# A decode attention block on one core: the query matrix to the head of SP's queue, x to ACT's, and half of one value set to GpSimd's queue

## The chip, the core and the metric

The kernel runs on one core of a Trainium2 chip. The metric is the device time of one execution in microseconds, where lower is better. A run of the profiler adds a record of every instruction, every DMA packet and every semaphore increment of one execution.

## The reference, cut to what matters

```python
def _A_ref(x, k_cache, v_cache, wq, wo):      # B=8, Sq=1, D=512, Hq=32, Hkv=8, Sk=4096, Dh=128
    W = min(4096, max(256, Sk // 4))          # 1024: the last 1024 positions alone
    q = (x @ wq).reshape(B, Sq, Hq, Dh).transpose(0, 2, 1, 3)
    k = jnp.repeat(k_cache[:, :, Sk - W:, :], rep, axis=1)     # rep = 4
    v = jnp.repeat(v_cache[:, :, Sk - W:, :], rep, axis=1)
    p = _softmax(jnp.einsum("bhqd,bhkd->bhqk", q, k) * (Dh ** -0.5), axis=-1)
    o = jnp.einsum("bhqk,bhkd->bhqd", p, v)
    return o.transpose(0, 2, 1, 3).reshape(B, Sq, Hq * Dh) @ wo
def _B_ref(x, w_gate, w_up, w_down):          # F = 1792
    return (_gelu(x @ w_gate) * (x @ w_up)) @ w_down

xn = _layernorm(A_x)
return A_x + _A_ref(xn, ...) * _silu(_B_ref(xn, ...))
```

All inputs are bf16. The attention window is 1024 positions of 8 batches and 8 key heads, so that keys and values are 16 MB each, `wq` and `wo` 4 MB each, and the three matrices of the feed-forward part 5.25 MB together.

## The kernel before, in words

The work is one pass over 47.46 MB that is read from HBM once. All large loads go through SP's queue, in the order in which the program issues them, into a ring of 19 slots of 1 MB (`slot`, 8 KB in each of 128 partitions). The order is: `x_sb`; four row blocks of `wq`; two of `w_gate` and two of `w_up`; the key sets K0 to K2; two halves of `w_down`; then V0, K3, V1, K4 and so on to V15 (`seq`, lines 404 to 415); and at the end `wo` in seven pieces of 512 KB and two of 256 KB (`load_wo`). A set is one key head and four batches, loaded as 32 groups of 32 positions by 4 batches (`load_set`, line 102), so 16 sets of keys (K) and 16 of values (V).

The first stage is the layer norm of x (lines 176 to 196: statistics on VectorE, a square root on ScalarE, four transposes on TensorE), then the query product (line 209) and the gate and up products (line 227). The main loop walks the key sets in quarters: transposes of the keys (line 289), copies out of PSUM by VectorE or ScalarE (lines 294, 296), scores (line 306), the maximum, the exponentials, the sums and the value product (line 368), each some steps behind the other. The last stage multiplies with `wo` (line 476), gates, adds x and stores four pieces.

x is read a second time, by four small loads of 8 rows by 128 columns each in ACT's queue (`xq_sb`, line 84). Only the last addition (line 486) uses it. GpSimd issues no DMA; it prepares constants by `select` (line 139) and is idle from 6 us on.

Completion semaphores are given out by the framework: eight for the DMAs of SP and ACT together, in the order of the program. A DMA waits until the one eight places before it has landed, and a load into a reused slot also waits for TensorE to have read it. So up to eight loads are under way at a time.

Of the kernel before, what the change touches and what calls it, by code (L numbers as in the profile page):

```python
# [11 lines left out]
BF16 = mybir.dt.bfloat16  # L12
# [5 lines left out]
def kernel(  # L18
# [13 lines left out]
    nc = tc.nc  # L32

    B, Sq, D = A_x.shape
    Hkv, Sk, Dh = A_k_cache.shape[1], A_k_cache.shape[2], A_k_cache.shape[3]
# [3 lines left out]
    win0 = Sk - W  # L39
    F = B_w_gate.shape[1]  # L40
    NDC = D // 128
    NFC = F // 128
    scale = float(Dh) ** -0.5
    P = nc.NUM_PARTITIONS
# [3 lines left out]
    G = 4  # L48
    NB = B // G
    NS = Hkv * NB  # L50
    KP = P // G
# [5 lines left out]
    NQB = D // 128  # L57
# [8 lines left out]
    rows = ctx.enter_context(tc.tile_pool(name="rows", bufs=1))  # L66
# [9 lines left out]


    x_sb = rows.tile([B, D], BF16, name="x_sb")
    nc.sync.dma_start(out=x_sb, in_=A_x.flatten_outer_dims())
    xq_sb = rows.tile([P, 128], BF16, name="xq_sb")  # L80
    nc.gpsimd.memset(xq_sb, 0.0)
    x_flat = A_x.flatten_outer_dims()
    for q in range(NQB):
        nc.scalar.dma_start(
            out=xq_sb[32 * q : 32 * q + B, :],
            in_=x_flat[:, q * 128 : (q + 1) * 128],
        )

    def slot():
        return ring.tile([P, SET], BF16, name="slot")  # L90

    def load_rows(w, r0, n, per, name):

        t = slot()
        cols = w.shape[1]
        nc.sync.dma_start(
            out=t[:, 0 : n * cols],
            in_=w.rearrange("(p k) n -> p k n", p=P)[:, r0 : r0 + n, :],
        )
        return t[:, 0 : n * cols].rearrange("p (k n) -> p k n", k=n)  # L100

    def load_set(cache, s):
        h, b0 = s // NB, (s % NB) * G
        t = slot()
        nc.sync.dma_start(
            out=t,
            in_=cache[b0 : b0 + G, h, win0:Sk, :].rearrange(
                "g (p c) d -> p g (c d)", p=KP
            ),
        )  # L110
        return t.rearrange("p (c d) -> p c d", c=NCH)

    def load_wo(h, r0, n):

        t = slot()
        nc.sync.dma_start(
            out=t[:, 0 : n * D],
            in_=A_wo[h * rep * Dh : (h + 1) * rep * Dh, :].rearrange(
                "(p r) n -> p r n", r=rep
            )[:, r0 : r0 + n, :],  # L120
        )
        return t[:, 0 : n * D].rearrange("p (r n) -> p r n", r=n)


    ident = consts.tile([P, P], BF16, name="ident")
# [31 lines left out]
    for r in range(rep):  # L157
        t = consts.tile([P, P], BF16, name=f"pick{r}")
# [3 lines left out]
    for i in range(3):  # L162
        t = consts.tile([P, NC], BF16, name=f"shift{i}")
# [17 lines left out]
    nc.vector.memset(eps_sb, 1e-5)  # L181
    rstd = rows.tile([B, 1], FP32, name="rstd")
    nc.scalar.activation(out=rstd, in_=mv[:, 1:2], func=ACT.Sqrt, bias=eps_sb, scale=1.0)
    nc.vector.reciprocal(out=rstd, in_=rstd)
    xhat = rows.tile([B, D], BF16, name="xhat")
    nc.vector.tensor_scalar(
        out=xhat, in0=x_sb, scalar1=mv[:, 0:1], scalar2=rstd[:, 0:1],
# [16 lines left out]

    q_ps = ps_sc.tile([P, Hq, B], FP32, name="sc")
    for k in range(NDC):
        w = load_rows(A_wq, k, 1, NDC, "wq")
        for m in range(Hq):
            nc.tensor.matmul(  # L209
                q_ps[:, m, :], w[:, 0, m * Dh : (m + 1) * Dh], xnT[:, k, :],  # L210
                start=(k == 0 and m == 0), stop=(k == NDC - 1 and m == Hq - 1),
                skip_group_check=True,
            )
    nc.vector.tensor_copy(
        out=qT, in_=q_ps.rearrange("p (h j) b -> p h b j", j=rep)
# [68 lines left out]
    K, V, kT, sc, pT, rec = {}, {}, {}, {}, {}, {}  # L284
# [132 lines left out]
    def fetch(kind, s):  # L417
        while True:
            k, i = pending.pop(0)
            if k == "K":  # L420
                K[i] = load_set(A_k_cache, i)
            elif k == "V":
                V[i] = load_set(A_v_cache, i)
            else:
                n = NFC // 2
                down_tiles.append(load_rows(B_w_down, i * n, n, NFC, "wd"))
            if (k, i) == (kind, s):
                return

    LV = 4 * (AHEAD - 1) + 2  # L430
    for t in range(QT * NS + LV + QT + 3):
        s, i = divmod(t, QT)
        if s < NS:
            if i == 0:
                fetch("K", s)
            transpose_quarter(s, i)
# [15 lines left out]
        if 0 <= s3 < NS:  # L452
            if i3 == 0:
                fetch("V", s3)
            value_quarter(s3, i3)
# [16 lines left out]
    for h, r0, n in parts:  # L472
        w = load_wo(h, r0, n)
        for r in range(r0, r0 + n):
            for q in range(NQB):
                nc.tensor.matmul(  # L476
                    s_ps[32 * q : 32 * q + B, :], oR[:, h, r, :],
                    w[:, r - r0, q * 128 : (q + 1) * 128],
                    start=(h == 0 and r == 0), stop=(h == Hkv - 1 and r == rep - 1),
                    skip_group_check=True,  # L480
                )
# [5 lines left out]
    for q in range(NQB):  # L487
        eng = nc.sync if q % 2 == 0 else nc.scalar
        eng.dma_start(
            out=o_flat[:, q * 128 : (q + 1) * 128], in_=out_sb[32 * q : 32 * q + B, :]  # L490
# [31 lines left out]
```

## Time and profile before

| | |
|---|---|
| median of 3 runs | 125.14 us (124.98 to 125.2) |
| the profiled execution | 125.09 us |
| its span in the profile | 123.2 us |
| TensorE, busy | 88.1 us (71%) |
| VectorE, busy | 68.9 us (56%) |
| ScalarE, busy | 45.9 us (37%) |
| GpSimd, busy | 4.9 us (4%) |
| bytes read from HBM | 47.46 MB, 385 GB/s over the span |
| chain that ended last | DMA 71%, TensorE 18%, VectorE 4% |

The span is the time from the first to the last instruction; 1.9 us of the execution lie around it. Times within the profile count from the start of the span. "SPq" and "ACTq" are the sequencers of SP and ACT that issue DMAs; q1 is SP's DMA queue and q10 ACT's. The queues of the kind "instruction" fetch program code. A DMA spreads over up to 16 DMA engines, and each of them adds one to its semaphore when its share has landed.

### The profile page before, as it was taken

The numbers are of one execution on the slowest core, as the hardware profiler recorded it, in microseconds if no ns is written. First come the engines' busy times: TensorE is split into PE (matmuls) and PEld (weight loads), VectorE is DVE, ScalarE is ACT, GpSimd is POOL, SyncE is SP. The second block draws the span as 40 slices with busy tenths as digits, with TensorE's granted clock in tenths as the row PEclk, the third lists the DMA queues.
The fourth block names the chain that finished last, engine by engine and source line by source line (L and its number), as shares of the span: only waits on it lengthen the run. The fifth ranks groups of instructions, "written<-read, shape, count | busy, mean of one in ns | idle before, by whom it ended". The sixth has DMA issues, their size and how long they took to land.

```text
span 123.2 us, 4592 instructions
## 1 busy us (share of the span) xinstructions
PE 88.1 (71%) x2044; PEld 79.1 (64%) x2044; DVE 68.9 (56%) x218; ACT 45.9 (37%) x54; POOL 4.9 (4%) x21
## 2 busy tenths in 40 slices
PE   0154338877995699989697979769889879855840
PEld 0143337876984688979586969658778668644720
DVE  5200100025577557978596879669679697875010
ACT  1300000053674426548254645346545565510000
POOL 7800000000000000000000000000000000000000
PEclk9999999999999999999999999999999999995595
DMA  3999999999999999999999999999999999999820
GB/s 67 411 426 431 424 410 421 421 415 423 425 420 415 418 412 423 412 418 415 420 420 423 418 415 420 418 415 412 423 418 418 415 423 415 408 398 410 320 92 3
DMA packets 7508, 47.77 MB, mean 388 GB/s; under 512 B 952, under 2 KB 960, under 8 KB 2880
## 3 DMA queue, kind: packets, MB, share of 16 engines
q1 hardware_dynamic: 7392, 47.46, 93.7%
q8 instruction: 16, 0.26, 0.9%
q14 instruction: 4, 0.03, 0.1%
q10 hardware_dynamic: 96, 0.01, 0.1%
HBM read 47.46 MB, written 0.01 MB: 385 GB/s over the span
## 4 chain that ended last, share of the span: by engine, by line
DMA 71%; PE 18%; DVE 4%; issue 3%; SPq 1%; DVEq 0%
DMA slot<-in_A_k_cache_dram 33%; DMA slot<-in_A_wo_dram 22%; DMA slot<-in_B_w_up_dram 12%; PE kT_ps L289 8%; DMA slot<-in_A_wq_dram 4%; PE sc L306 3%; PE o_ps L368 3%; PE sum_ps L351 1%; PE m_ps L322 1%; PE sc L340 1%; DVE kT L294 1%; PE s L265 1%; DVE mx L315 1%; DVE rec L356 1%; DVE oR L398 1%
## 5 line engine op out<-in xcount | busy, mean ns | idle before, releaser
L289 PE MATMUL kT_ps<-ident,slot 128*128 128x128 bf16 x512 | 40.8, 226 | 6.1 <-DMA slot<-in_A_k_cache_dram 5.1
L296 ACT ACTIVATE kT<-kT_ps 128x1024 bf16<-128x1024 bf16 x32 | 32.7, 1023 | 23.9 <-PE kT_ps L289 22.3
L289 PEld LDWEIGHTS <-slot 128*128 128x128 bf16 x512 | 31.0, 100 | 7.4 <-DMA slot<-in_A_k_cache_dram 5.8
L368 PEld LDWEIGHTS <-slot 128*128 128x128 bf16 x512 | 20.5, 96 | 10.4 <-issue 5.7
L294 DVE COPY kT<-kT_ps 128x1024 bf16<-128x1024 bf16 x32 | 21.6, 675 | 8.1 <-PE kT_ps L289 8.1
L368 PE MATMUL o_ps<-pT,slot 128*128 128x16 bf16 x512 | 22.0, 170 | 2.6 <-DVE oT L374 1.2
L306 PE MATMUL sc<-qT,kT 128*128 128x16 bf16 x512 | 22.7, 170 | 0.7 <-issue 0.6
L306 PEld LDWEIGHTS <-kT 128*128 128x128 bf16 x512 | 19.9, 97 | 0.9 <-issue 0.8
L346 ACT ACTIVATE pT<-sc 128x512 bf16<-128x512 f32 x16 | 9.6, 597 | 16.0 <-PE sc L340 16.0
L315 DVE TENSOR_REDUCE mx<-sc 128x16 f32<-128x512 f32 x16 | 11.1, 691 | 5.6 <-PE sc L306 5.3
L356 DVE TENSOR_REDUCE rec<-sum_ps 128x16 f32<-128x512 f32 x16 | 11.1, 691 | 3.5 <-PE sum_ps L351 3.1
L227 PE MATMUL sc<-xnT,slot 128*128 128x8 bf16 x112 | 7.4, 202 | 3.6 <-DMA slot<-in_B_w_gate_dram 2.9
L227 PEld LDWEIGHTS <-slot 128*128 128x128 bf16 x112 | 7.1, 161 | 3.9 <-DMA slot<-in_B_w_gate_dram 3.1
L238 ACT ACTIVATE z<-sc 128x112 f32<-128x112 f32 x1 | 0.3, 264 | 21.4 <-PE sc L227 21.4
L209 PE MATMUL sc<-xnT,slot 128*128 128x8 bf16 x128 | 4.1, 168 | 5.3 <-DMA slot<-in_A_wq_dram 5.3
L209 PEld LDWEIGHTS <-slot 128*128 128x128 bf16 x128 | 3.7, 104 | 5.7 <-DMA slot<-in_A_wq_dram 5.7
L351 PE MATMUL sum_ps<-pT,ones 128*128 128x512 bf16 x16 | 6.2, 389 | 0.7 <-issue 0.7
L340 PE MATMUL sc<-shift,spread 68*128 68x512 bf16 x16 | 6.0, 376 | 1.0 <-DVE kT L294 0.9
L322 PE MATMUL m_ps<-identf,mx 128*16 128x128 f32 x16 | 4.4, 275 | 2.7 <-DVE kT L294 1.3
L239 DVE TENSOR_SCALAR z<-z 128x112 f32<-128x112 f32 x1 | 0.2, 218 | 10.8 <-ACT z L238 10.8
L398 DVE CAST oR<-m_ps 32x32 bf16<-32x32 f32 x32 | 5.8, 183 | 0.7 <-PE m_ps L388 0.4
L476 PE MATMUL s<-slot,oR 128*8 128x128 bf16 x128 | 3.9, 285 | 2.5 <-DMA slot<-in_A_wo_dram 1.3
(58 smaller groups left out, 47.1 us busy)
## 6 DMA issues: line engine op xcount, KB each, us to landing
slot<-in_A_k_cache_dram SPq DMA_DIRECT2D x16, 1024.0 KB, 20.1
slot<-in_A_v_cache_dram SPq DMA_DIRECT2D x16, 1024.0 KB, 19.8
slot<-in_A_wq_dram SPq DMA_DIRECT2D x4, 1024.0 KB, 7.9
slot<-in_A_wo_dram SPq DMA_DIRECT2D x7, 512.0 KB, 18.6
slot<-in_B_w_gate_dram SPq DMA_DIRECT2D x2, 896.0 KB
slot<-in_B_w_up_dram SPq DMA_DIRECT2D x2, 896.0 KB
slot<-in_B_w_down_dram SPq DMA_DIRECT2D x2, 896.0 KB
slot<-in_A_wo_dram SPq DMA_DIRECT2D x2, 256.0 KB, 9.2
```

Of the source, the lines that this page charges most:

```text
L209: nc.tensor.matmul(q_ps[:, m, :], w[:, 0, m * Dh : (m + 1) * Dh], xnT[:, k, :], start=(k == 0 and m == 0), stop=(k == NDC - 1 and m == Hq ...
L227: nc.tensor.matmul(gu_ps[:, j, w, :], wv[:, k, j, :], xnT[:, k0 + k, :], start=(w == 0 and k0 == 0 and j == 0 and k == 0), stop=(w == 1 an ...
L289: nc.tensor.transpose(ps[:, c * P : (c + 1) * P], K[s][:, i * CQ + c, :], ident)
L294: nc.vector.tensor_copy(out=t, in_=ps)
L296: nc.scalar.activation(out=t, in_=ps, func=ACT.Copy)
L306: nc.tensor.matmul(sc[s][:, i * CQ + c, :], t[:, c * P : (c + 1) * P], q, start=(i == 0 and c == 0), stop=False, skip_group_check=True,)
L315: nc.vector.tensor_reduce(out=m, in_=sc[s].rearrange("p c n -> p n c"), axis=AX.X, op=ALU.max)
L340: nc.tensor.matmul(sc[s].rearrange("p c n -> p (c n)"), spread[0:SHK, :], r[0:SHK, :].unsqueeze(1).to_broadcast([SHK, NCH, NC]), start=Fal ...
L346: nc.scalar.activation(out=t, in_=sc.pop(s), func=ACT.Exp, scale=scale)
L351: nc.tensor.matmul(ps.rearrange("p c n -> p (c n)"), ones, pT[s].rearrange("p c n -> p (c n)"), start=True, stop=True,)
L356: nc.vector.tensor_reduce(out=t, in_=ps.rearrange("p c n -> p n c"), axis=AX.X, op=ALU.add)
L368: nc.tensor.matmul(o_ps[s].rearrange("p g j -> p (g j)"), V[s][:, c, :], pT[s][:, c, :], start=(c == 0), stop=(c == NCH - 1),)
```

## The change

`x_sb` is loaded by ACT instead of SP, so that the first block of `wq` is the first load in SP's queue; all four blocks are issued ahead of the constants. The four loads of `xq_sb`, and the clearing of that tile, come after the square root of the layer norm. V7 is loaded in three pieces instead of one: two loads of 32 partitions in GpSimd's queue, each behind a load of 8 rows by 2 by 64 elements of x into a tile that nothing reads (`turn`), and one load of the other 64 partitions in SP's queue. The large loads of GpSimd wait for the slot of K0 to be free; the value product of set 7 waits for all three.

```diff
-    nc.sync.dma_start(out=x_sb, in_=A_x.flatten_outer_dims())
-    xq_sb = rows.tile([P, 128], BF16, name="xq_sb")
-    nc.gpsimd.memset(xq_sb, 0.0)
-    x_flat = A_x.flatten_outer_dims()
-    for q in range(NQB):
-        nc.scalar.dma_start(
-            out=xq_sb[32 * q : 32 * q + B, :],
-            in_=x_flat[:, q * 128 : (q + 1) * 128],
-        )
+    nc.scalar.dma_start(out=x_sb, in_=A_x.flatten_outer_dims())
...
+    turn = [rows.tile([B, 2, 96], BF16, name=f"turn{i}") for i in range(2)]
+
+    def load_set(cache, s, split=False):
         h, b0 = s // NB, (s % NB) * G
         t = slot()
...
+        src = cache[b0 : b0 + G, h, win0:Sk, :].rearrange(
+            "g (p c) d -> p g (c d)", p=KP
+        )
+        n = 0
+        if split:
+            for i in range(2):
+                m = KP // 4
+                nc.gpsimd.dma_start(
+                    out=turn[i][:, :, 0:64],
+                    in_=x_flat.rearrange("b (i n) -> b i n", i=2)[:, :, 0:64],
+                )
+                nc.gpsimd.dma_start(
+                    out=t[n * G : (n + m) * G, :], in_=src[n : n + m]
+                )
+                n += m
+        nc.sync.dma_start(out=t[n * G : P, :], in_=src[n:KP])
         return t.rearrange("p (c d) -> p c d", c=NCH)
...
+    wq_tiles = [load_rows(A_wq, k, 1, NDC, "wq") for k in range(NDC)]
...
     nc.scalar.activation(out=rstd, in_=mv[:, 1:2], func=ACT.Sqrt, bias=eps_sb, scale=1.0)
+
+    xq_sb = rows.tile([P, 128], BF16, name="xq_sb")
+    nc.gpsimd.memset(xq_sb, 0.0)
+    x_flat = A_x.flatten_outer_dims()
+    for q in range(NQB):
+        nc.scalar.dma_start(
+            out=xq_sb[32 * q : 32 * q + B, :],
+            in_=x_flat[:, q * 128 : (q + 1) * 128],
+        )
...
     for k in range(NDC):
-        w = load_rows(A_wq, k, 1, NDC, "wq")
+        w = wq_tiles[k]
...
             elif k == "V":
-                V[i] = load_set(A_v_cache, i)
+                V[i] = load_set(A_v_cache, i, (k, i) == ("V", 7))
```

More of the change, by code (lines that the diff above doesn't have):

```diff
@@ L100, in load_rows @@
         return t[:, 0 : n * cols].rearrange("p (k n) -> p k n", k=n)
-    def load_set(cache, s):
+    turn = [rows.tile([B, 2, 96], BF16, name=f"turn{i}") for i in range(2)]
+    def load_set(cache, s, split=False):
         h, b0 = s // NB, (s % NB) * G
         t = slot()
[L105 to L109, printed above, removed]
-        )
+        src = cache[b0 : b0 + G, h, win0:Sk, :].rearrange(
+            "g (p c) d -> p g (c d)", p=KP
+        )
+        n = 0
[11 more added lines that the diff above has]
+        nc.sync.dma_start(out=t[n * G : P, :], in_=src[n:KP])
         return t.rearrange("p (c d) -> p c d", c=NCH)
```

## The prediction, made before the changed kernel ran

> **What bounds the kernel now.** I read the DMA part of the page first, then the end of the chain of waits.
>
> ```profile
> DMA  3999999999999999999999999999999999999820
> GB/s 67 411 426 431 424 410 421 421 415 423 425 420 415 418 412 423 412 418 415 420 420 423 418 415 420 418 415 412 423 418 418 415 423 415 408 398 410 320 92 3
> ...
> q1 hardware_dynamic: 7392, 47.46, 93.7%
> q8 instruction: 16, 0.26, 0.9%
> q14 instruction: 4, 0.03, 0.1%
> q10 hardware_dynamic: 96, 0.01, 0.1%
> ```
>
> The DMA engines are full from slice 2 to slice 37: TensorE's 71% costs nothing while data come at this rate. The chain in order of time ends in DMA as well:
>
> ```profile
> 91.77 18.61 DMA slot<-in_A_wo_dram
> ...
> 110.44 8.89 DMA slot<-in_A_wo_dram
> 119.33 0.04 issue
> 119.38 0.31 PE s L476 x8
> ```
>
> So only two things move the end: when the stream starts, and when the last DMA engine finishes. The busy time by stretches says that they don't finish together (the last two columns are DMA share and GB/s):
>
> ```profile
> 110.00:115.00 5.00, 2.33 (x65) 1.99 (x69) 2.70 (x12) 0.00 (x0) 0.00 (x0) 0.55 1.04 410
> 115.00:116.00 1.00, 1.00 (x48) 1.00 (x40) 0.00 (x0) 0.00 (x0) 0.00 (x0) 0.50 0.84 324
> 116.00:117.00 1.00, 0.87 (x40) 0.67 (x32) 0.00 (x0) 0.00 (x0) 0.00 (x0) 0.50 0.60 236
> 117.00:118.00 1.00, 0.40 (x16) 0.20 (x7) 0.00 (x0) 0.00 (x0) 0.00 (x0) 0.86 0.47 180
> 118.00:119.00 1.00, 0.67 (x24) 0.39 (x24) 0.00 (x0) 0.00 (x0) 0.00 (x0) 1.00 0.33 117
> ```
>
> The last load of `wo` shows the same: of its 16 increments nine come at 115.81 to 117.91 us and seven at 118.90 to 119.33.
>
> **Who is late.** The records of single packets tell why. In the steady stream an engine moves 8 KB in 309 ns and its next packet follows within 4 ns, so the packets join into 16 chains. Queue q8's sixteen fetches of 16 KB take 0.96 to 1.11 us each, and the packet behind one mostly takes 0.8 us instead of 0.31: some 1.5 us lost to that engine. They go round eight chains in fixed order (15.1, 25.8, 37.5, 44.9, 50.8, 57.1, 63.4, 69.6 us, then the first again at 75.7). Chains hit twice are late by some 3 us (one load ends at 102.6 to 103.3 us on chains never hit, at 105.7 to 106.2 on those hit twice).
>
> Which eight? An 8-row load runs on eight engines (q10's 96 packets are four loads and two stores, each of 8 data and 8 semaphore packets). The loads of `xq_sb` mark their eight chains at 5.1 to 7.2 us. Followed to the fetches, four of those hit are marked ones and four are not. One of the marked could be swapped with another chain that starts its packets in the same nanoseconds; so it is at least three on each side. Among the late seven at the end are three marked and four others.
>
> **The change, part by part.**
>
> *The start.* The view by time:
>
> ```profile
> 0.73 0.39 SPq L79 DMA_DIRECT2D x_sb<-in_A_x_dram  x1
> 0.96 1.62 ACTq L84 DMA_DIRECT2D xq_sb<-in_A_x_dram  x4
> 1.18 1.93 SPq L96 DMA_DIRECT2D slot<-in_A_wq_dram  x4
> 2.30 0.68 DVE L177 BATCH_NORM_STATS2 stats<-x_sb 8x6 f32<-8x512 bf16 x1 [0.47 <-DMA x_sb<-in_A_x_dram]
> ```
>
> Without the load of x ahead, the first `wq` block is issued at 0.73 instead of 1.18: the stream starts **0.45 us** earlier (bounds 0.39, the issue alone, and 0.45; I take 0.45). Everything behind it in SP's queue moves along.
>
> *x behind `wq`.* ACT issues x at about 0.96, and its packets reach engines that have begun the first `wq` block. The nearest row is the second load of `xq_sb`, issued about 1.36: its packets came only at 5.1, behind that block, and it landed at 5.6 to 6.2. So x lands near 5.7 instead of 2.3. From the statistics to the first query product (6.03) it took 3.73 us, of which 0.7 was ScalarE's table load (2.62 to 3.90), now done under the wait: the product starts near 8.7. Cover: a block takes 1.02 us of TensorE and they land 2.5 us apart, the last at 13.5, or 13.1 now; three before it need 3.1, so a start up to 10.0 costs nothing. Slack 1.3 us: cost 0. Without it each late microsecond delays the gate product, which itself waits 2.7 us for its load: still hidden.
>
> *`xq_sb`.* Its four issues (1.62 us) now stand behind the square root in ACT's queue, near 7; ACT's next work is line 238, at 25 us. Semaphores shift by the new order: gate's first block waits for the first `wq` block (landing near 5.5) with 3 MB still queued, 7.5 us of stream; K0 waits for the first of `xq_sb`, landed by 11, before its turn at 13. The memset of 0.20 on GpSimd moves behind the selects. All 0.
>
> *V7.* SP's piece keeps 64 partitions, 32 KB on each of 16 engines instead of 64 KB. The other 512 KB come from GpSimd when K0's slot is free, at 31 us (the end of its transposes), behind one small load each; SP issued V7 at 52.9, so these are early, and GpSimd has nothing else to do. No row shows a GpSimd DMA. By the nearest rows, the 8-row loads, a load with eight shares uses eight engines: 32 KB each, and both large loads on the same eight if the small ones take the other eight in turn: 64 KB. Then eight engines carry 32 KB more than before, four packets of 309 ns, **+1.24 us**, and eight carry 1.24 us less. The lower bound is 0: both loads spread evenly. Upper: if GpSimd cuts rows into 256-byte packets (15 ns each in q10's rows), 64 KB take 3.84 instead of 2.47 us: +2.6. I take 1.24: 8 KB rows are moved whole everywhere in this trace.
>
> The Trainium skill (DMA: Bandwidth & Descriptors, on why a DMA increments its semaphore by 16) says that a GpSimd DMA with eight shares takes eight consecutive engines from a cursor that goes round. By that rule both large loads do fall on one half; no row here shows it.
>
> With late engines in both halves, the loaded half has them whichever half it is. The end is the latest engine: 119.33 - 0.45 + 1.24 = 120.12, **+0.79 us**. Relief of the other half is worth nothing. From 31 to about 73 us the loaded engines lag by 2.47, so sets land up to 2.0 us later there; eight loads are under way (20 us from issue to landing), so the stream doesn't run dry, and TensorE's delay has until 110 to vanish.
>
> The profiled execution took 125.09, 0.05 under the median of 125.14: 125.09 + 0.79 = **125.9**.
>
> **Rivals.**
>
> 1. *Relief.* The loaded eight are exactly the eight that q8 never hits. Then the late ones end at 119.33 - 1.24 = 118.09, the others at up to 117.51 + 1.24 = 118.75, and the end is 118.75 - 0.45 = 118.30, 1.03 earlier: **124.1**. It decides as soon as no fetched engine is in the loaded half. For it: 512 KB moved is close to what levels 3 us. Against: the marks of `xq_sb`, if GpSimd's eight are cut as ACT's eight are. Chance 0.28.
> 2. *No shift.* GpSimd's loads use all 16 engines or alternate halves; only the start counts: 125.09 - 0.45 = **124.6**. Against: eight leading shares. Chance 0.07. The same skill page, in its section that issuing engines are not separate DMA queues, says that loads from any engine share the same 16 and that a change of issuer saves only issue time; by that the time would be this one, too.
> 3. *Small packets* from GpSimd: +2.6 - 0.45 on late engines, **127.2**. Chance 0.05.
>
> **The numbers.** About 0.2%, 0.25 us, is what can be told from no change. Forecast 0.57, with its own range 125.5 to 126.5 (a lower end if the extra packets fall on engines whose second fetch comes late; the upper if TensorE's delay remains in part). Slower: 0.57 + 0.05 = 0.62. Faster: 0.28 + 0.07 = 0.35. Same: 0.03, where the halves differ by chance. The range 124.0 to 126.5 leaves out the small packets and tails.
>
> **What would show it.** In the profile after: `wq` first in SP's queue at about 0.73; the first query product between 8 and 9.5 with no later wait for it; a third queue with some 64 packets of 8 KB after 31 us; line 476's last wait ending near 120.1, and a DMA share above 0.2 from 118 to 120. I am wrong if the increments of the last `wo` load draw together and end near 118.3 (relief), or keep today's spread 0.45 earlier (no shift); and if the query product ends after the gate blocks are in, the start was not free.

## The result, and the profile after

The changed kernel took **131.4 us** (median of five runs, 131.21 to 131.77) against 125.14 us (124.98 to 125.2) for the kernel before: a ratio of 1.0506, 95% interval 1.0491 to 1.0521. The direction was forecast, the size was not: 6.3 us slower instead of 0.8, far above the range's upper end of 126.5. Its profiled execution took 131.48 us with a span of 129.6.

The page's DMA part shows where. This is the busy share and the rate of the DMA engines in 40 slices of 3.24 us each, and the queues:

```profile
DMA  3999999999999999999999999999999999999510
GB/s 116 430 425 420 416 422 420 417 413 422 386 279 286 351 420 420 415 422 407 417 425 399 240 313 407 422 417 415 420 412 425 410 427 406 407 401 393 228 69 3
...
q1 hardware_dynamic: 7312, 46.93, 91.7%
q0 software_dynamic: 224, 0.53, 1.5%
```

The row of nines is as unbroken as it was before: by the busy share nothing has happened. The row below it has two holes, slices 11 to 14 (386, 279, 286, 351) and 22 to 24 (399, 240, 313). The engines are busy and move less, so in these stretches a packet takes longer. The view by stretches puts them beside TensorE. Behind the stretch and its length stand the busy times of TensorE, of its weight loads, of VectorE, ScalarE and GpSimd; the last three columns are granted clock, DMA share and GB/s:

```profile
20.00:33.00 13.00, 10.78 (x163) 10.37 (x161) 3.68 (x9) 4.52 (x6) 1.66 (x3) 1.00 1.01 419
33.00:46.00 13.00, 6.30 (x113) 5.29 (x110) 5.11 (x15) 4.06 (x5) 0.00 (x0) 0.72 1.02 325
46.00:69.00 23.00, 21.98 (x490) 19.77 (x489) 16.35 (x49) 11.29 (x14) 0.00 (x0) 0.79 1.01 418
69.00:79.00 10.00, 7.83 (x189) 7.08 (x187) 7.42 (x24) 4.86 (x6) 0.00 (x0) 1.00 1.02 318
79.00:110.00 31.00, 27.81 (x640) 25.32 (x639) 24.30 (x77) 16.70 (x20) 0.00 (x0) 0.94 1.01 417
```

The same two stretches of the kernel before, from the same view:

```profile
33.00:46.00 13.00, 10.24 (x243) 9.00 (x241) 8.50 (x24) 6.51 (x8) 0.00 (x0) 1.00 1.02 420
69.00:79.00 10.00, 8.28 (x202) 7.60 (x202) 7.73 (x24) 5.38 (x7) 0.00 (x0) 1.00 1.01 415
```

The first hole holds GpSimd's two loads: the 64 data packets of 8 KB in q0 begin between 34.6 and 43.7 us. The second lies between 71 and 76 us; no packet of q0 is left there, and it fits SP's 64-partition piece of V7, issued at 57.9 us with some 15 to 21 us from issue to landing. Packet by packet, an 8 KB packet that took 309 ns before (the shortest; the median is 312) takes about 540 ns (median from 36.5 to 38 us) and 614 ns (median from 71 to 73 us). I add up what all 8 KB packets took beyond 309 ns and divide by 16 engines: from 33 to 46 us that is 3.10 us against 0.25 before, from 69 to 79 us 2.57 against 0.20. So the two holes cost every engine **2.85 and 2.37 us** on average.

Most of it is paid by other loads. From 69 to 79 us 157 packets took over 400 ns (two before), and the piece of V7 has only 64. From 33 to 46 us 230 did, and GpSimd's 64 packets (mean 446 ns) bear 8.7 of the 49.6 us lost.

The chain in order of time ends as before, in the last piece of `wo`, only later (landing 125.58 instead of 119.33, 6.25 us):

```profile
116.73 8.85 DMA slot<-in_A_wo_dram
125.58 0.04 issue
125.62 0.31 PE s L493 x8
```

This landing can be summed up: 119.33 before, -0.45 for the start, +2.85 and +2.37 for the holes, +1.24 for the unevenly loaded engines gives 125.34; 0.24 is left over. The last load also shows the uneven engines themselves: its 16 increments came within 3.52 us before (115.81 to 119.33) and within 6.02 now (119.56 to 125.58). The end by stretches, same columns as above:

```profile
118.00:119.00 1.00, 1.00 (x26) 0.72 (x27) 0.23 (x1) 0.00 (x0) 0.00 (x0) 0.50 1.01 397
...
120.00:122.00 2.00, 0.85 (x28) 0.82 (x31) 0.94 (x6) 0.00 (x0) 0.00 (x0) 0.50 0.70 272
122.00:124.00 2.00, 2.00 (x84) 1.96 (x73) 0.00 (x0) 0.00 (x0) 0.00 (x0) 0.50 0.38 141
124.00:126.00 2.00, 1.12 (x40) 0.49 (x31) 0.05 (x1) 0.00 (x0) 0.00 (x0) 0.99 0.18 60
```

The start, by time:

```profile
0.74 0.59 ACTq L79 DMA_DIRECT2D x_sb<-in_A_x_dram  x1
0.74 2.05 SPq L88 DMA_DIRECT2D slot<-in_A_wq_dram  x4
...
2.79 0.68 DVE L185 BATCH_NORM_STATS2 stats<-x_sb 8x6 f32<-8x512 bf16 x1 [0.96 <-DMA x_sb<-in_A_x_dram]
...
5.57 1.02 PE L226 MATMUL sc<-xnT,slot 128*128 128x8 bf16 x32 [0.52 <-DMA slot<-in_A_wq_dram]
```

and GpSimd's issues, by time:

```profile
30.80 0.57 POOL L112 DMA_DIRECT2D slot<-in_A_v_cache_dram  x1 [23.89 <-PE kT_ps L306]
31.36 0.55 POOL L108 DMA_DIRECT2D turn<-in_A_x_dram  x1
31.90 0.56 POOL L112 DMA_DIRECT2D slot<-in_A_v_cache_dram  x1
```

### The profile page after: what moved, and what is told of

It reads as the page before. It is cut to its first block, busy times and chain, and to the rows that moved or that the text cites. A ratio compares the mean times of both kernels' runs of the same rounds, so it can differ in the third digit from the quotient of the medians.

```text
span 129.6 us, 4601 instructions
## 1 busy us (share of the span) xinstructions
PE 92.7 (72%) x2044; PEld 83.3 (64%) x2044; DVE 68.7 (53%) x218; ACT 46.0 (35%) x54; POOL 7.2 (6%) x25
## 4 chain that ended last, share of the span: by engine, by line
DMA 58%; PE 28%; DVE 7%; issue 3%; SPq 1%; ACT 0%; DVEq 0%
DMA slot<-in_A_k_cache_dram 36%; PE kT_ps L306 13%; DMA slot<-in_B_w_up_dram 8%; DMA slot<-in_A_wo_dram 7%; DMA slot<-in_A_wq_dram 7%; PE o_ps L385 4%; PE sc L323 4%; PE sc L357 2%; DVE mx L332 2%; DVE kT L311 1%; PE m_ps L339 1%; PE sum_ps L368 1%; PE s L282 1%; DVE rec L373 1%; SPq L88 1%
## 5 line engine op out<-in xcount | busy, mean ns | idle before, releaser
L306 PE MATMUL kT_ps<-ident,slot 128*128 128x128 bf16 x512 | 44.5, 238 | 5.7 <-DMA slot<-in_A_k_cache_dram 3.4
L306 PEld LDWEIGHTS <-slot 128*128 128x128 bf16 x512 | 33.7, 106 | 7.2 <-DMA slot<-in_A_k_cache_dram 3.6
L385 PEld LDWEIGHTS <-slot 128*128 128x128 bf16 x512 | 21.1, 98 | 13.8 <-issue 5.7
L385 PE MATMUL o_ps<-pT,slot 128*128 128x16 bf16 x512 | 22.5, 171 | 6.7 <-DMA slot<-in_A_v_cache_dram 4.6
L323 PEld LDWEIGHTS <-kT 128*128 128x128 bf16 x512 | 20.7, 99 | 0.0
L244 PEld LDWEIGHTS <-slot 128*128 128x128 bf16 x112 | 7.0, 159 | 3.7 <-DMA slot<-in_B_w_gate_dram 2.9
L226 PEld LDWEIGHTS <-slot 128*128 128x128 bf16 x128 | 3.7, 104 | 5.4 <-DMA slot<-in_A_wq_dram 5.4
L368 PE MATMUL sum_ps<-pT,ones 128*128 128x512 bf16 x16 | 6.7, 416 | 0.8 <-issue 0.8
L357 PE MATMUL sc<-shift,spread 68*128 68x512 bf16 x16 | 6.5, 404 | 0.9 <-DVE kT L311 0.8
```

Source lines behind the costliest of these rows:

```text
L226: nc.tensor.matmul(q_ps[:, m, :], w[:, 0, m * Dh : (m + 1) * Dh], xnT[:, k, :], start=(k == 0 and m == 0), stop=(k == NDC - 1 and m == Hq ...
L244: nc.tensor.matmul(gu_ps[:, j, w, :], wv[:, k, j, :], xnT[:, k0 + k, :], start=(w == 0 and k0 == 0 and j == 0 and k == 0), stop=(w == 1 an ...
L306: nc.tensor.transpose(ps[:, c * P : (c + 1) * P], K[s][:, i * CQ + c, :], ident)
L323: nc.tensor.matmul(sc[s][:, i * CQ + c, :], t[:, c * P : (c + 1) * P], q, start=(i == 0 and c == 0), stop=False, skip_group_check=True,)
L357: nc.tensor.matmul(sc[s].rearrange("p c n -> p (c n)"), spread[0:SHK, :], r[0:SHK, :].unsqueeze(1).to_broadcast([SHK, NCH, NC]), start=Fal ...
L368: nc.tensor.matmul(ps.rearrange("p c n -> p (c n)"), ones, pT[s].rearrange("p c n -> p (c n)"), start=True, stop=True,)
```

## The experiments

The theory after the result: a load that covers only part of the partitions can set two DMA engines writing to the same place in SBUF, and then both move at half their speed. Below, "places" are the parts of SBUF that one engine writes in a load of all 128 partitions. The Trainium skill (SBUF — State Buffer, Door 1: The DMA port swizzle) has such places: partitions 0 to 63 are reached through eight of 16 ports and 64 to 127 through the other eight, so that 64 partitions get the rate of 32. The trace agrees with the factor: twice 309 ns is 618, and the second hole's median is 614.

The rivals: the start costs something; the extra bytes on eight engines cost more than thought; GpSimd's queue itself slows the others; the loads come too early and disturb the key sets. All ratios are against the kernel before on the same chip, whose medians were 125.05 to 125.18 us.

### The two parts alone

`e1_start_only` keeps the new start and loads V7 as before; `e8_split_only` has the old start and V7 in three pieces.

```diff
 # e1, from the changed kernel
-                V[i] = load_set(A_v_cache, i, (k, i) == ("V", 7))
+                V[i] = load_set(A_v_cache, i)
 # e8, from the kernel before
-                V[i] = load_set(A_v_cache, i)
+                V[i] = load_set(A_v_cache, i, (k, i) == ("V", 7))
```

> Only the first part of the change: the query matrix first in SP's queue, x and its four copies in ACT's; V7 is one load in SP's queue again. In the changed kernel the first block of wq landed at 5.52 us instead of 5.98, and the stream ran at its old rate until 33 us. All theories of the split say that this part alone gains about 0.45 us: 124.7 us against 125.14. If the new order of semaphores or x behind the first block costs something, it is 125.0 or more.

> Only the second part of the change: V7 in three pieces as in the changed kernel, the start as before. If the parts are independent it is the changed kernel's 131.4 plus 0.45: 131.85 us. If the start and the split disturb each other (the shorter queue at the start), it is clearly less.

Measured: e1 124.76 us (124.61 to 125.0), ratio 0.9972 [0.9961, 0.9984]; e8 131.48 us (131.27 to 131.72), ratio 1.0508 [1.0494, 1.0522]. The whole loss is in V7's pieces, and the start is a small gain. In e1 the last `wo` landed at 118.83, 0.50 earlier than before. Its rate row has no hole:

```profile
GB/s 96 427 427 425 426 413 422 426 416 414 419 420 413 424 416 424 416 419 413 421 405 424 416 421 416 427 413 421 411 419 413 419 419 416 409 400 416 315 89 3
```

The parts don't add up exactly: e8 was expected 0.45 above the changed kernel and came within 0.1 of it, so beside the split the new start is worth hardly anything; why was not tested.

### Pieces of 64 partitions, without GpSimd

`e2_sp_halves` has the new start and loads V7 as two pieces of 64 partitions, both by SP.

```diff
...
+            h2 = KP // 2
+            nc.sync.dma_start(out=t[0 : h2 * G, :], in_=src[0:h2])
+            nc.sync.dma_start(out=t[h2 * G : P, :], in_=src[h2:KP])
...
```

> The changed start; V7 in two loads of 64 partitions, both in SP's queue, no DMA from GpSimd. Theory A (places): a load that spans only part of the 128 partitions makes two DMA engines write through one entrance of SBUF; then each half costs what SP's half cost in the changed kernel (its packets of 8 KB from 69 to 79 us took 2.37 us more in the mean over 16 engines than in the same stretch before): 124.7 + 4.7 = 129.4 us, and packets of about 600 ns. Theory B (GpSimd): loads through GpSimd's queue slow the others; then there is nothing to pay here: 124.7 us.

Measured: 128.26 us (128.12 to 128.29), ratio 1.0248 [1.0234, 1.0262]. Same queue, same bytes on each engine, same order; only the shape differs from e1, and it costs 3.5 us. The page has one hole, where V7 lands, and the view by stretches gives it at full DMA share:

```profile
GB/s 106 430 428 423 418 418 425 422 409 423 415 430 410 428 410 423 405 430 407 425 410 340 226 283 410 428 415 420 418 412 425 415 415 415 408 403 410 296 84 3
```

```profile
68.00:74.00 6.00, 4.42 (x82) 3.95 (x81) 3.83 (x14) 2.05 (x3) 0.00 (x0) 0.79 1.03 233
```

So the shape alone does it. Two pieces side by side cost 3.1 us of packet time, not twice 2.37; why they cost less together was not settled. The last `wo` landed at 122.33, against 119.33 - 0.45 + 3.1 = 121.98.

### The same bytes by GpSimd, in all partitions

`e3_gp_columns` gives GpSimd the same 512 KB as half of the columns of all 128 partitions.

```diff
...
+            c2 = SET // 2
+            nc.gpsimd.dma_start(out=t[:, 0:c2], in_=src[:, :, 0:c2])
+            nc.sync.dma_start(out=t[:, c2:SET], in_=src[:, :, c2:SET])
...
```

> The changed start; the same 512 KB of V7 in GpSimd's queue as in the change, but cut by columns: one load of all 128 partitions by 4 KB through GpSimd and one of all 128 partitions by 4 KB through SP, no small loads. Theory A (places): every engine keeps its partitions, nothing slows: 124.7 us, 8 KB packets next to it at 0.31 us. Theory B (GpSimd): the stretch in which GpSimd's load runs slows as from 34 to 44 us in the changed kernel, 2.85 us: 127.5 us.

Measured: 124.95 us (124.83 to 125.76), ratio 0.9994 [0.9979, 1.0008]. GpSimd's 128 packets of 4 KB took 164 ns on average, and the stretch that was the first hole runs at full rate:

```profile
33.00:46.00 13.00, 9.43 (x180) 8.17 (x177) 6.67 (x19) 5.60 (x7) 0.00 (x0) 0.72 1.02 421
```

GpSimd's queue is not to blame for the hole, nor is cutting V7 into two loads. The time lies 0.19 us above e1 and the last landing 0.22 (119.05 against 118.83); no run shows why.

### GpSimd's loads in the other half

`e4_gp_upper` sends GpSimd's two loads to partitions 64 to 127 and SP's piece to 0 to 63.

```diff
+        n = KP if not split else KP // 2
...
-                    out=t[n * G : (n + m) * G, :], in_=src[n : n + m]
+                    out=t[(n + i * m) * G : (n + (i + 1) * m) * G, :],
+                    in_=src[n + i * m : n + (i + 1) * m],
...
-        nc.sync.dma_start(out=t[n * G : P, :], in_=src[n:KP])
+        nc.sync.dma_start(out=t[0 : n * G, :], in_=src[0:n])
```

> The change, with the halves of V7 swapped: GpSimd's two loads (each behind its small one) go to partitions 64 to 95 and 96 to 127, SP's load to partitions 0 to 63. Bytes, queues and shares stay. Theory A (places), if GpSimd's eight engines are those that write the upper partitions in a load of 128: the first slow stretch (34 to 44 us) goes, SP's half (2.4 us) stays, and so does the uneven load of 1.24: 124.7 + 2.4 + 1.2 = 128.3 us. Theory A with the other eight engines, and theory B (GpSimd): 131.4 us as in the change.

Measured: 128.17 us (128.06 to 129.22), ratio 1.0266 [1.0231, 1.0301]. One hole of two is gone. GpSimd's packets take 313 ns on average instead of 446:

```profile
33.00:46.00 13.00, 8.89 (x163) 7.59 (x162) 6.67 (x18) 5.65 (x7) 0.00 (x0) 0.76 1.02 418
68.00:74.00 6.00, 4.73 (x119) 4.25 (x116) 3.98 (x13) 3.15 (x4) 0.00 (x0) 1.00 1.05 317
```

Nothing was changed but the half of the partitions, and with it the rows of V7 that are read for them. So, by the theory, GpSimd's eight engines are those whose places are partitions 64 to 127: there they write undisturbed, while in the changed kernel they write into the places of the other eight. The last `wo` landed at 122.33; 118.88 (119.33 less the start) + 2.28 for the hole that is left (4.48 us beyond 309 ns for each engine in the whole run, 2.20 in e1) + 1.24 for the loaded engines is 122.40. The profiled execution (129.22) is the longest of the four; in it TensorE multiplied with `wo` without a pause from 119.40 to 123.27 and so ended 0.9 us behind the landing.

### Every engine in its own places

`e5_own_places` goes on from e4: SP's half is loaded as two pieces of 32 partitions, that is of eight shares each.

```diff
-        nc.sync.dma_start(out=t[0 : n * G, :], in_=src[0:n])
+            for i in range(2):
+                nc.sync.dma_start(
+                    out=t[i * m * G : (i + 1) * m * G, :], in_=src[i * m : (i + 1) * m]
+                )
...
```

> As the run before, but SP's half of V7 is two loads of 32 partitions with eight shares each (partitions 0 to 31 and 32 to 63) instead of one of 64 partitions with sixteen. If eight shares of SP run on the eight engines that write partitions 0 to 63 in a load of 128, and GpSimd's on the other eight, every engine writes its own partitions and moves the same bytes as in one load of V7. Theory A (places): no slow stretch and no uneven load, 124.7 us. Theory B (GpSimd): 127.5 us or more. If the engines are other ones than I think: 128 us or more.

Measured: 126.24 us (125.65 to 126.5), ratio 1.008 [1.0052, 1.0109]. No hole is left (time of the 8 KB packets beyond 309 ns, for each engine in the whole run, 2.14 us against 2.21 before), GpSimd's packets take 315 ns, and the last `wo` landed at 119.15. The rows and the partitions of every byte are those of e4; only the way in which SP's half is dealt out to the engines differs. So the rows that are read don't make the hole. Nor does the size of a piece alone: GpSimd's loads of 32 partitions have a hole in the changed kernel and none in e4. But the end came 1.5 us later than e1's. The chain no longer ends in a load:

```profile
114.69 0.70 DVE rec L376
117.34 3.61 PE s L496 x98
```

TensorE is late. It was set back between 38 and 48 us, at half the granted clock:

```profile
38.00:48.00 10.00, 6.76 (x117) 5.89 (x118) 2.58 (x6) 2.64 (x3) 0.00 (x0) 0.50 1.01 419
```

Just before and in this stretch it waited for a value set and for a key set:

```profile
38.79 0.38 PE L388 MATMUL o_ps<-pT,slot 128*128 128x16 bf16 x8 [1.96 <-DMA slot<-in_A_v_cache_dram]
42.48 1.04 PE L309 MATMUL kT_ps<-ident,slot 128*128 128x128 bf16 x8 [1.60 <-DMA slot<-in_A_k_cache_dram]
```

From 30 to 50 us these are all its waits for loads, 3.6 us; in e1 it is one wait of 1.1 us. It did not catch up. The waits of TensorE from 48 to 117 us, in e1, show what there is to catch up with (waited in total, times, longest, in us):

```profile
PE kT_ps L306 <- DMA slot<-in_A_k_cache_dram: 3.7, 5, 1.0
```

In e5 the same view has no wait for a load: TensorE is behind the loads up to 117 us, and waits only within its own chain, for VectorE and its own issue.

The bytes of V7 that GpSimd fetches at 35 us delay the sets that are due then. `e9_own_places_later` holds GpSimd's loads until 54.25 us, by a small copy of a result that exists only then:

```diff
+            hold = rows.tile([P, rep, G], BF16, name="hold")
+            nc.gpsimd.tensor_copy(out=hold, in_=oT[:, 1, :, 0:G])
```

> As the run with own places (126.24 us), but GpSimd first copies a small column that set 2's value product leaves at about 54 us, so that its two loads of V7 start there and not at 31 us, near the turn of SP's half. In the run with own places the last load of wo landed at 118.5 us, as in the run with the start only, and the end came 2.5 us later, out of TensorE's chain: TensorE was busy 6.8 of 10 us from 38 to 48 at half clock and never free after it. Theory C (early bytes): the 512 KB moved at 34 to 41 us make eight engines, and so every key set that waits for them, 2.5 us late while TensorE waits for keys: then 124.7 to 125.0 us here. If the loads cost TensorE its time whenever they run: 126.2 us.

Measured: 125.12 us (124.96 to 125.44), ratio 0.9999 [0.999, 1.0007]. (The 118.5 that the expectation names is the landing of the last load but one.) The early bytes cost e5 its 1.1 us; the stretch is whole again:

```profile
38.00:48.00 10.00, 8.01 (x224) 7.30 (x223) 6.87 (x21) 4.50 (x6) 0.00 (x0) 1.00 1.00 415
```

What remains, 0.36 us above e1, is mostly in the landing (119.17 against 118.83) and has no cause shown. Nor did any run separate how much of e5's setback is missing data and how much the halved clock. That the clock alone is not enough is likely: in e3 it was 0.53 from 38 to 48 us, with 2.1 us of waits for loads from 30 to 50 us, and e3 ended at 124.95.

### Is it the early start in the changed kernel, too?

`e10_change_later` puts the same two lines into the changed kernel.

> The changed kernel, with GpSimd held back in the same way to about 54 us or later. Theory A (places) and the uneven load, which set the end by the last load of wo, stay: 131.4 us, with the first slow stretch moved to 55 to 65 us. If the early start is what costs the change its time (theory C alone): 128 us or less.

Measured: 131.8 us (131.57 to 132.07), ratio 1.0539 [1.0521, 1.0557]. The first hole moves with GpSimd's loads, from 34 to 44 us to 60 to 69 us, joins the second, and nothing is gained:

```profile
GB/s 114 430 427 422 414 420 425 417 415 420 427 410 425 417 422 415 410 417 372 289 281 346 230 314 427 410 427 415 417 417 420 417 417 408 411 402 389 217 70 3
```

### Without the small loads

`e11_no_turn` drops the loads into `turn`, so that GpSimd's two large loads follow each other.

```diff
-                nc.gpsimd.dma_start(
-                    out=turn[i][:, :, 0:64],
-                    in_=x_flat.rearrange("b (i n) -> b i n", i=2)[:, :, 0:64],
-                )
```

> The changed kernel without the two small loads of GpSimd. If eight shares go round the sixteen engines, the load of partitions 0 to 31 runs on the eight engines that write these in a load of 128, and the load of partitions 32 to 63 on the other eight: the first slow stretch costs half (1.4 instead of 2.85 us), the load is even (no 1.24), SP's half stays (2.4): the last load of wo lands at 118.9 + 1.4 + 2.4 = 122.7 and the time is 128.5 us. If both run on the same eight: 131.4 us, or 130 and less without the uneven engines being those that clash.

Measured: 128.79 us (128.58 to 129.17), ratio 1.0297 [1.0279, 1.0315]. The first hole has shrunk to 1.3 us and is over just before 40 us, and the 1.24 us of unevenly loaded engines is gone (the increments of the last load come within 3.50 us, as before the change):

```profile
GB/s 116 426 432 420 419 418 421 421 415 417 426 341 313 419 421 411 426 411 421 411 424 414 274 261 411 424 416 414 421 408 429 411 426 406 408 401 412 313 89 3
```

That is what comes out if the second load takes the other eight engines: one of the two then writes in its own engines' places. GpSimd's packets show the switch: the first 28 large ones (34.7 to 36.3 us) took 309 to 320 ns, the 36 behind them 335 to 544. The Trainium skill (DMA: Bandwidth & Descriptors, Why a DMA increments its semaphore by 16 and not by 1) says that a GpSimd load with eight shares takes eight consecutive engines from a cursor that goes round; e4 and e11 agree. So the small load of eight, put ahead of each large one, is what sends both to the same eight engines, and with partitions 0 to 63 as their target these were the wrong eight.

### Which half of the engines is late?

`e6_extra_upper` and `e7_extra_lower` have the new start, V7 as in e1, and one load of 256 KB by GpSimd that nothing uses, on the one or the other eight engines, in these engines' own places.

```diff
 # e6, after the constants
+    extra = rows.tile([P, SET], BF16, name="extra")
+    nc.gpsimd.dma_start(out=turn[0][:, :, 0:64], in_=x_flat.rearrange("b (i n) -> b i n", i=2)[:, :, 0:64])
+    nc.gpsimd.dma_start(out=extra[64 : 64 + 32, :], in_=...[0 : KP // 4])
 # e7: without the load into turn, and
-    nc.gpsimd.dma_start(out=extra[64 : 64 + 32, :], in_=...[0 : KP // 4])
+    nc.gpsimd.dma_start(out=extra[0 : 0 + 32, :], in_=...[0 : KP // 4])
```

> The changed start with V7 in one load, and beside it 256 KB that nothing uses: one load of 32 partitions (64 to 95) with eight shares in GpSimd's queue, behind one small load of eight, at the start of the stream. It is the uneven load of the change alone: 32 KB more on eight engines, none less on the others. The prediction's claim (late engines in both halves): four packets of 309 ns on late engines, 124.7 + 1.24 = 125.9 us. If those eight engines are never late at the end: 124.7 to 124.9.

> As the run before, with the 256 KB on the other eight engines: partitions 0 to 31 and no small load ahead. The prediction's claim (late engines in both halves): 125.9 us here as well. If all late engines are in the half that the change relieved: 125.9 here and 124.7 to 124.9 in the run before; if GpSimd's count starts at another engine, both are mixed and show slow packets.

Measured: e6 125.8 us (125.76 to 125.91), ratio 1.0059 [1.0046, 1.0071]; e7 125.95 us (125.84 to 126.16), ratio 1.0074 [1.006, 1.0088]. The last `wo` landed at 119.87 and 120.01, that is 1.04 and 1.18 us behind e1's 118.83, for four packets of 309 ns (1.24) on eight engines. Their packets took 309 ns on average. Both halves have late engines, and 32 KB on either half moves the end.

## Why the prediction was wrong, and where it was right

**The step that failed** is the cost of V7, as the prediction put it: SP's piece "keeps 64 partitions, 32 KB on each of 16 engines instead of 64 KB", and GpSimd's loads are "64 KB" on eight engines, all of it in packets of 309 ns. It counted bytes for each engine and took the duration from loads of all 128 partitions; it asked which engines read, and not where they write. No row of before had an 8 KB packet of a load of 64 or of 32 partitions. The bound for such a shape should have been asked for. The section of the Trainium skill named above (SBUF — State Buffer, Door 1: The DMA port swizzle) gave a rival by its rule: 64 partitions at the rate of 32. In its place the runs show +2.85 us for GpSimd's two loads and +2.37 us for SP's piece: 125.9 + 5.2 = 131.1 of the 131.4 measured. So the direction came out for the forecast reason only in its smaller part, 0.8 of 6.3 us. The upper bound had looked only at the size of the packets, and all of GpSimd's large ones were 8 KB, as forecast.

**The engines loaded unevenly** were right: "+1.24". Each half has late engines (e6, e7), so relief, the first rival at 0.28, falls. The lag of the loaded engines, foretold as 2.47 us, shows as 6.02 - 3.52 = 2.50 us more spread in the last load. The rival "no shift" fell as a forecast of the time. With it fell the time that the prediction drew from the rule of the Trainium skill (DMA: Bandwidth & Descriptors, Issuing engines are not separate DMA queues) that a change of issuer saves only issue time; e3 agrees with the rule itself, since there the issuer changed, the load kept all 128 partitions, and the time stayed within 0.2 us of e1.

**The start** was right, -0.45: the first `wq` block was issued at 0.74 and landed at 5.52 instead of 5.98, and e1's time came out 0.28% (0.38 us) lower; beside the split it showed hardly at all (e8). The step on x was wrong at no cost. Its landing was put near 5.7, behind the first `wq` block; VectorE began on it at 2.79. ACT issued it at 0.74, not 0.96, since the loads of `xq_sb`, from whose time the 0.96 was taken, had waited for a clearing by GpSimd; x's packets ran from 1.71 us, just ahead of `wq`'s first at 1.78. The nearest row was the first of those loads, not the second: its packets had come at 1.93 us. The 3.73 us from the statistics to the product also held some 0.65 us in which the product waited for its block of `wq`. The query product began at 5.57 instead of 8.7.

**The small edits** at zero (`xq_sb`, semaphores, the clearing) hold: e1 contains them all and gained 0.50 us in the last landing.

**"TensorE's delay has until 110 to vanish"** was wrong as a general cover. In e5 the delay never vanished and the early bytes cost 1.1 us, as e9 shows. In the changed kernel it didn't matter, since the loads ended still later (e10).

**What would show it:** the third queue after 31 us was there with its 64 packets of 8 KB, among 224 in all, most of the rest of 4 bytes; the last wait was at 125.58 instead of 120.1. The hole in the rate at full DMA share was on no list, and it was the sign.

Of all kernels here e1 is the fastest: the new start with V7 in one load.

## What to carry to other kernels

When a load is cut up, keep every piece on all 128 partitions and cut along the columns (e3: within 0.2 us of the load in one piece). Cutting along the partitions cost 1.3 to 2.9 us of packet time for each 512 KB here (e11, e2, the two holes), most of it paid by other loads, except where each engine wrote in its own places (e5). Read the rate row beside the busy row: busy engines at a falling rate mean longer packets, and the first place to look is which engines write to which partitions. And a transfer that runs early takes its bytes from what is due then; on a kernel with little idle time the bound engine may not get them back (e5 against e9).

## What was not expected of the hardware

- A load of 64 partitions over 16 engines took 8 KB packets from 309 to 614 ns (median from 71 to 73 us), for all loads under way at the time: 157 slow packets for a piece of 64.
- Eight-share loads run at full speed (309 to 315 ns) when their engines write in their own places, and slow the others down when they write in another's (446 ns for their own, about 540 for all around). That it is the engine's place that decides is inferred from e4, e5 and e11; the trace does not number the engines.
- A GpSimd load posts more packets than its data: 224 in q0, of which 64 are of 8 KB, 32 belong to the small loads, and 128 are of 4 bytes.
- TensorE's granted clock was 0.50 from 38 to 48 us in e5 (1.00 in e9), and on average 0.72 from 33 to 46 us in the changed kernel and also in e3, which has no hole (0.87 in e1, 1.00 in the kernel before). What sets it off was not tested.
